# Weight loads on ScalarE's queue, and some normalisations on GpSimd, in a fused attention and gated-MLP kernel

## The chip, the cores and the metric

One core of one Trainium2 chip. The metric is the device time of one execution in microseconds (us), lower is better. The kernel before took 271.23 us (median of 3 runs, 269.55 to 272.23). TensorE is PE in the profile, its weight loads PEld, VectorE is DVE, ScalarE is ACT, GpSimd is POOL, and SyncE, which issues most transfers, is SP. A name with q (SPq, ACTq) is the engine's own instruction queue. A hole is a stretch in which TensorE has no matmul to run. An eviction copies a matmul's result out of psum, the accumulator. A crossbar transpose is a DMA transfer that transposes a tile on its way; here it brings a normalised tile from tring to xh, the input of the next matmuls. The clock is the share of TensorE's full clock that was granted.

## The reference, cut to what matters

```python
# x: 1 x 2048 x 448, bf16; 16 heads of 28; window of 8 keys, dilation 2
h  = x + attention(layernorm(x)) @ wo              # LN1, q/k/v, sliding window, wo
# gated MLP, F = 1792, Fh = 896
z  = gelu(layernorm(h) @ w_in)                     # LN2
z1 = z[..., :Fh]
z2 = layernorm(z[..., Fh:])                        # LN3, over 896
g  = einsum('ts,bsf->btf', w_sp, z2) + b_sp        # w_sp is 2048 x 2048
out = h + (z1 * g) @ w_out
```

There are three normalisations. LN1 and LN2 work on 16 blocks of 128 tokens by 448, LN3 on 16 blocks of 128 by 896. The last product with w_sp needs every block of LN3 before its first accumulation is complete.

## The kernel before

The program is a list of tasks with a duration, a priority and dependencies; a list scheduler (the planner) turns it into a fixed instruction order for each engine. A task may have `alts`: engines that can do it, each with a duration. The planner gives the task to whichever engine is free in its model.

```python
# planner, cut
if t.alts:
    for x in t.alts:
        ready[x].remove(t)
    t.eng = e
    t.dur = t.alts[e]
...
def ln_unit(u, which, src_deps, prio, ev_deps):      # LN1 and LN2: two blocks, u and u + 8
    ... # bn_stats, bn_aggr on VectorE
    tr = add("rs%d_%d" % (which, u), "pool", 1.05, em_r, deps=tb, prio=prio)   # 1/sqrt on GpSimd
    for n, b in enumerate(bl):
        def em_n(b=b, n=n):
            iss("dve", lambda e: e.tensor_scalar(tring[:, h[0], :]..., x_tm[:, b, :]...,
                     mv[:, b, 0:1], rs[:, b:b + 1], ALU.subtract, ALU.mult), ...)
        tn.append(add("nrm%d_%d" % (which, b), "dve", 0.41, em_n, ...))
    if which == 2 or u >= NPET:                      # crossbar transpose into xh
        return dma("sp", "tD%d_%d" % (which, u), lambda e: e.dma_start(
            xh[...], tring[:, h[0], :], transpose=True), ...)
...
t_wo.append(dma("sp", "wo%d" % hh, ...))             # 4 loads, one resource r_wo
ld_win(1, 2.0); ld_win(0, 2.4)                       # 8 loads, dma("sp", ...)
...
# LN3: rstd on GpSimd for a pair of blocks, then for each of the two
iss("dve", lambda e: e.tensor_scalar(z2p[:, b, :], z2p[:, b, :], mv3[:, b, 0:1], rs3[:, b:b + 1],
                                     ALU.subtract, ALU.mult), ...)
t_z2[b] = add("nrm3_%d" % b, "dve", 0.43, em, deps=[tp], ...)
...
pace = [by[n % i] for i in range(NT) for n in ("exp%d_0", "mask%d", "ot%d")]
chain(t_win[1] + t_win[0] + [t_wsp[b][0] for b in S_ORDER], pace)   # each load waits for a step and the load before
```

The softmax here doesn't subtract the row's maximum and nothing guards it: scores larger than these inputs give would overflow.

## Time and profile before

| | before |
|---|---|
| time, median | 271.23 us |
| profiled span, mean clock of the matmul engine | 270.2 us, 0.968 |
| PE / DVE / ACT / POOL busy | 250.4 / 150.5 / 88.5 / 33.5 us |
| first w_sp matmul | 149.51 us |
| PE idle from 8.76 to 149.5 us | 13.8 us |

A group line reads: source line, engine, operation, output <- inputs, shape, count, then busy us in all and mean ns of one, then the idle time of the engine just before. Kernel before, groups by form:

```profile
L668 DVE TENSOR_SCALAR tring<-x_tm,mv,rs 128x448 bf16<-128x448 bf16 x32 | 15.2, 492 | 4.3 <-POOL rs L648 4.3
L1033 DVE TENSOR_SCALAR z2p<-z2p,mv,rs 128x896 bf16<-128x896 bf16 x16 | 7.4, 501 | 1.1 <-POOL rs L648 1.1
L1084 PE MATMUL psum<-wspT_lo,z2p 128*128 128x512 bf16 x219 | 48.1, 379 | 0.4 <-issue 0.2
```

All 32 normalisations of LN1 and LN2 (line 668) and all 16 of LN3 (line 1033) run on VectorE at about 0.5 us each. None of them is on GpSimd. The first half of the w_sp matmuls (line 1084), which needs the results of LN3, is idle for 0.4 us in all.

### The profile page before, as it was taken

What the parts mean: (1) busy time and instruction counts of PE and PEld (TensorE: products, weight loads), DVE (VectorE), ACT (ScalarE), POOL (GpSimd) and SP (SyncE); (2) the same over time, 40 slices, a digit from 0 to 9 for tenths busy, and PEclk for the clock granted to TensorE, in tenths of its full rate; (3) what the DMA queues carried; (4) which work ended last, traced back from release to release, by engine and by line L of the source; (5) the groups of instructions that cost most, each with busy time, mean ns of one, the idle gap of its engine ahead of it and who ended that gap; (6) DMA issues with size and microseconds to landing.
All of it is one profiled execution on the core that took longest, in us unless ns stands there. A gap on an engine that the chain in (4) does not pass through costs nothing.

```text
span 270.2 us, 6513 instructions
## 1 busy us (share of the span) xinstructions
PE 250.4 (93%) x2912; PEld 126.0 (47%) x2922; DVE 150.5 (56%) x281; ACT 88.5 (33%) x97; POOL 33.5 (12%) x80
## 2 busy tenths in 40 slices
PE   7698967999969897989999999999999999999995
PEld 2275533445635444345555444444444444444442
DVE  3878861585784688599997133342334333334333
ACT  1458721737635745967667100000000000000000
POOL 7652200000211013113322000000000000000000
PEclk9979995999997999799999999999999999999999
DMA  7903495423275946659953434433000200010002
GB/s 207 281 26 66 102 166 107 109 53 70 67 103 115 98 96 75 114 101 168 222 87 80 77 86 95 90 80 107 0 0 2 68 0 0 2 51 17 0 2 68
DMA packets 55412, 22.03 MB, mean 82 GB/s; under 512 B 46664, under 2 KB 55256, under 8 KB 55384
## 3 DMA queue, kind: packets, MB, share of 16 engines
q1 hardware_dynamic: 54376, 20.40, 37.8%
q10 hardware_dynamic: 1008, 1.20, 1.6%
q8 instruction: 23, 0.38, 0.6%
q14 instruction: 5, 0.04, 0.1%
HBM read 8.39 MB, written 1.84 MB: 38 GB/s over the span
## 4 chain that ended last, share of the span: by engine, by line
PE 85%; DVE 4%; DMA 4%; POOL 3%; ACT 1%; issue 1%; POOLq 0%
PE psum L1084 36%; PE psum L790 11%; PE psum L988 9%; PE psum L1113 8%; PE psum L1047 8%; PE psum L830 5%; DMA xh<-tring 4%; PE psum L865 3%; PE psum L968 2%; PE psum L914 2%; ACT reg L642 1%; DVE reg L644 1%; DVE reg L932 1%; DVE tring L668 1%; PE psum L894 1%
## 5 line engine op out<-in xcount | busy, mean ns | idle before, releaser
L1094 DVE TENSOR_TENSOR ub<-psum,reg 128x512 bf16<-128x512 f32 x28 | 19.4, 692 | 68.9 <-PE psum L1084 68.9
L1084 PE MATMUL psum<-reg,z2p 128*128 128x512 bf16 x219 | 48.4, 379 | 0.3
L1084 PE MATMUL psum<-wspT_lo,z2p 128*128 128x512 bf16 x219 | 48.1, 379 | 0.4 <-issue 0.2
L1084 PEld LDWEIGHTS psum<-wspT_lo,z2p 128*128 128x128 bf16 x224 | 21.8, 98 | 26.6 <-issue 0.4
L1084 PEld LDWEIGHTS psum<-reg,z2p 128*128 128x128 bf16 x224 | 21.9, 98 | 26.3
L790 PE MATMUL psum<-xh,reg 64*128 64x128 bf16 (+3 forms) x336 | 29.6, 327 | 3.8 <-DMA xh<-tring 3.8
L988 PE MATMUL psum<-w_in,xh 64*128 64x448 bf16 x224 | 26.1, 380 | 5.0 <-DMA xh<-tring 3.5
L642 ACT ACTIVATE reg<-psum 128x896 bf16<-128x896 f32 (+5 forms) x23 | 18.7, 841 | 17.9 <-PE psum L747 6.5
L644 DVE CAST reg<-psum 128x896 bf16<-128x896 f32 (+4 forms) x14 | 15.1, 1076 | 14.0 <-PE psum L790 9.6
L878 ACT ACTIVATE reg<-psum 128x928 bf16<-128x928 f32 x18 | 16.9, 944 | 16.8 <-PE psum L865 7.4
L1113 PE MATMUL psum<-reg 128*128 128x448 bf16 x112 | 22.0, 352 | 0.0
L1047 PE MATMUL psum<-xh,w_in 64*128 64x512 bf16 x196 | 21.9, 376 | 0.0
L647 POOL TENSOR_SCALAR rs<-mv 128x2 f32<-128x2 f32 x24 | 7.8, 326 | 109.2 <-DVE mv L658 90.9
L790 PEld LDWEIGHTS psum<-xh,reg 64*128 64x128 bf16 x336 | 14.4, 99 | 14.5 <-issue 7.2
L657 DVE BATCH_NORM_STATS2 st<-x_tm 128x6 f32<-128x448 bf16 x32 | 19.5, 610 | 1.9 <-DMA x_tm<-in_A_x_dram 1.8
L988 PEld LDWEIGHTS psum<-w_in,xh 64*128 64x128 bf16 x224 | 11.8, 100 | 15.4 <-DMA xh<-tring 3.9
L668 DVE TENSOR_SCALAR tring<-x_tm,mv,rs 128x448 bf16<-128x448 bf16 x32 | 15.2, 492 | 4.3 <-POOL rs L648 4.3
L1019 DVE BATCH_NORM_STATS2 st<-z2p 128x6 f32<-128x448 bf16 x32 | 17.4, 598 | 0.0
L648 POOL TENSOR_TENSOR rs<-rs,nhalf 128x2 f32<-128x2 f32 x24 | 17.0, 708 | 2.0
L1057 ACT ACTIVATE reg<-psum 128x1024 bf16<-128x1024 f32 x14 | 14.3, 1024 | 7.2 <-PE psum L1047 7.2
L830 PE MATMUL psum<-reg,xh 64*64 64x448 bf16 x252 | 14.7, 373 | 1.6 <-DVE xh L644 1.0
L1113 PEld LDWEIGHTS psum<-reg 128*128 128x128 bf16 x112 | 11.0, 98 | 10.5
(65 smaller groups left out, 213.4 us busy)
## 6 DMA issues: line engine op xcount, KB each, us to landing
w_in<-in_B_w_in_dram SPq DMA_DIRECT2D x4, 448.0 KB, 5.2
out_dram<-tring SPq DMA_DIRECT2D x16, 112.0 KB, 1.7
x_tm<-in_A_x_dram SPq DMA_DIRECT2D x15, 112.0 KB, 6.1
w_in<-in_B_w_in_dram SPq DMA_DIRECT2D x4, 336.0 KB, 4.1
reg<-in_B_w_out_dram SPq DMA_DIRECT2D x1, 784.0 KB, 5.4
z2p<-in_A_wqkv_dram ACTq DMA_DIRECT2D x1, 672.0 KB, 4.9
reg<-in_B_b_sp_dram SPq DMA_DIRECT2D x1, 512.0 KB, 6.1
reg<-in_A_wqkv_dram ACTq DMA_DIRECT2D x1, 392.0 KB, 7.0
```

The lines of the kernel that those rows point to most:

```text
L642: iss("act", lambda e: e.activation(dst, src, AF.Copy), reads=rd, writes=wr)
L644: iss(eng, lambda e: e.tensor_copy(dst, src), reads=rd, writes=wr)
L657: iss("dve", lambda e: e.bn_stats(st[:, b, :], x_tm[:, b, :]), reads=[r_x[b]], writes=[rl[b]])
L668: iss("dve", lambda e: e.tensor_scalar(tring[:, h[0], :].rearrange("p (c s f) -> p s c f", c=NC7, s=2)[:, n], x_tm[:, b, :].rearrange("p ( ...
L790: iss("pe", lambda e, c=c, s=s, gi=gi, lhs=lhs: e.matmul(psum[:, bk[s] * 512 + cw * gi:bk[s] * 512 + cw * gi + cw], lhs, xh[64 * s:64 * s ...
L830: iss("pe", lambda e, c=c, s=s, w=w: e.matmul(psum[64 * w:64 * w + 64, bk[s] * 512:bk[s] * 512 + D], xh[64 * s:64 * s + 64, c, XO - HALO + ...
L988: iss("pe", lambda e, c=c, s=s: e.matmul(psum[:, zb[s] * 512:zb[s] * 512 + D], xh[64 * s:64 * s + 64, c, XO + 128 * u:XO + 128 * u + 128], ...
L1019: iss("dve", lambda e, b=b: e.bn_stats(st3[:, b, k, :], z2p[:, b, D * k:D * k + D]), reads=[r_z2[b][k]], writes=[r_st3[b][k]])
L1047: iss("pe", lambda e, c=c, s=s: e.matmul(psum[:, bk[s] * 512:bk[s] * 512 + 512], w_in[64 * s:64 * s + 64, c, 128 * f:128 * f + 128], xh[64 ...
L1084: iss("pe", lambda e, b=b: e.matmul(psum[:, gb[0] * 512:gb[0] * 512 + 512], z2p[:, b, 128 * f:128 * f + 128], src[:, b, 512 * (tc % 2):512 ...
L1094: iss("dve", lambda e: e.tensor_tensor(ub[:, us_[0], :], psum[:, gb[0] * 512:gb[0] * 512 + 512], bb[:, 512 * tc:512 * tc + 512], ALU.add), ...
L1113: iss("pe", lambda e, f=f: e.matmul(psum[:, wb[0] * 512:wb[0] * 512 + D], z1p[f][:, 128 * m:128 * m + 128], w_out[:, f, :], start=(f == 0) ...
```

## The change

Its intent is to keep SyncE's in-order queue free for the crossbar transposes that feed the matmuls: the wo and w_in loads are issued by ScalarE, wo is tracked as four parts, and the w_sp loads wait for a compute step only. In addition, normalisations may go to GpSimd, to relieve VectorE. The offsets and the seed of the planner were searched again, and it was told new issue times for the transposes (`issue=1.3`, `issue=1.2`, `bw=200.0`; not shown in the cut).

```diff
-MPEN = 5.115
-OFF = {"q": -60.45, ...}
-SEED, SIGMA = 953666, 1.0
+MPEN = 2.853
+OFF = {"q": -91.78, ...}
+SEED, SIGMA = 570774, 1.0
...
-        r_wo = Res("wo")
+        r_wo = [Res("wo%d" % i) for i in range(4)]
...
-                    t = dma("sp", "win%d_%d%d" ...
+                    t = dma("act", "win%d_%d%d" ...
...
-                    iss("dve", lambda e: e.tensor_scalar(tring...
+                    iss(tn[n].eng, lambda e: e.tensor_scalar(tring...
-                              acq=[] if n else [("tr", 1, h)]))
+                              acq=[] if n else [("tr", 1, h)], alts={"dve": 0.41, "pool": 0.65}))
...
-            t_wo.append(dma("sp", "wo%d" % hh, ...  prio=1.0 + 0.01 * hh, writes=[r_wo]
+            t_wo.append(dma("act", "wo%d" % hh, ... prio=-310 + 0.01 * hh, writes=[r_wo[hh]]
-        ld_win(1, 2.0); ld_win(0, 2.4)
+        ld_win(1, -300.0); ld_win(0, -299.0)
...
-                    iss("dve", lambda e: e.tensor_scalar(z2p[:, b, :], ...
+                    iss(tk[0].eng, lambda e: e.tensor_scalar(z2p[:, b, :], ...
-                t_z2[b] = add("nrm3_%d" % b, "dve", 0.43, ...)
+                t_z2[b] = add("nrm3_%d" % b, "dve", 0.43, ..., alts={"dve": 0.43, "pool": 1.05})
...
-        chain(t_win[1] + t_win[0] + [t_wsp[b][0] for b in S_ORDER], pace)
+        pace = [t_x[NB - 1]] + [by["mm%s1_%d" % (p, g)] for g in range(4) for p in "kq"]
+        chain(t_win[1] + t_win[0], pace, False)       # order in the plan only, no real wait
+        pace = [by[n % i] for i in range(2, NT) for n in ("exp%d_0", "mask%d", "ot%d")]
+        chain([t_wsp[b][0] for b in S_ORDER], pace)
```

With the durations 0.65 and 1.05 us, the planner put 24 of the 32 small normalisations and 8 of the 16 large ones on GpSimd.

More of the change, by code (lines that the diff above doesn't have):

```diff
@@ L35 @@
 WPEN = 200
-MPEN = 5.115
-OFF = {"q": -60.45, "v": -24.73, "evv": 46.46, "l": -68.6, "exp": 40.78, "mask": -30.77, "r": -72.61,
-       "o": -92.46, "ln": 28.79, "ot": 3.99, "y": 5.48, "h": 16.73, "ln2": -52.4, "zr": 73.75, "z2": 10.47,
-       "ge": -61.49, "n3": 62.79, "x0": -17.97, "xd": 1.56, "evq": 43.13}
-SEED, SIGMA = 953666, 1.0
+MPEN = 2.853
+OFF = {"q": -91.78, "v": -31.46, "evv": 70.84, "l": -101.63, "exp": 9.21, "mask": -63.08, "r": -105.01,
+       "o": -160.47, "ln": -77.16, "ot": -5.85, "y": -22.31, "h": -36.55, "ln2": -0.64, "zr": 155.82,
+       "z2": 10.2, "ge": -30.33, "n3": 78.44, "x0": -71.31, "xd": 55.9, "evq": 48.9}
+SEED, SIGMA = 570774, 1.0
 O_AFTER_LN = True
@@ L501, in bass_sequential_preLN__sliding_local_dilated__mixer_gmlp__prompt_kernel @@
         reg2_old = [r for rr in r_q + r_k for r in rr] + [r_qend, r_kend] + r_OT
-        reg3_old = [r_wo] + [r for e2 in r_E for r in e2] + r_L + r_V
+        reg3_old = r_wo + [r for e2 in r_E for r in e2] + r_L + r_V
         EP_TILE, EP_UNIT = {}, {}
@@ L571, in ld_win @@
                 for c0, c1 in ((0, 4), (4, 7)):
-                    t = dma("sp", "win%d_%d%d" % (z, s, c0), lambda e, s=s, c0=c0, c1=c1: e.dma_start(
+                    t = dma("act", "win%d_%d%d" % (z, s, c0), lambda e, s=s, c0=c0, c1=c1: e.dma_start(
                         w_in[64 * s:64 * s + 64, c0:c1, FH * z:FH * z + FH],
@@ L667, in em_n @@
                 def em_n(b=b, n=n):
-                    iss("dve", lambda e: e.tensor_scalar(tring[:, h[0], :].rearrange("p (c s f) -> p s c f", c=NC7, s=2)[:, n],
+                    iss(tn[n].eng, lambda e: e.tensor_scalar(tring[:, h[0], :].rearrange("p (c s f) -> p s c f", c=NC7, s=2)[:, n],
                                                          x_tm[:, b, :].rearrange("p (c f) -> p c f", c=NC7),
@@ L676, in ln_unit @@
                     xh[:, :, XO + 128 * u:XO + 128 * u + 128], tring[:, h[0], :], transpose=True), 128 * 896 * 2,
-                    deps=tn + list(ev_deps), prio=prio + 1.0 - 600, reads=LazyRes(r_tr, h), writes=[r_xh[u]], rel=[("tr", h)])
+                    deps=tn + list(ev_deps), prio=prio + 1.0 - 600, reads=LazyRes(r_tr, h), writes=[r_xh[u]], rel=[("tr", h)], issue=1.3, bw=200.0)
             bk = []
@@ L726, in bass_sequential_preLN__sliding_local_dilated__mixer_gmlp__prompt_kernel @@
                 t_xpad = add("evh", "dve", 0.17, em_e, deps=[th], prio=3.25, rel=[("ps", hb)])
-        c_wo0 = cst("c_wo0", [(lambda e: e.memset(wo_p[:, :, :], 0.0), [], [r_wo])], 1.65, prio=50, deps=[t_xh[1]])
+        c_wo0 = cst("c_wo0", [(lambda e: e.memset(wo_p[:, :, :], 0.0), [], r_wo)], 1.65, prio=50, deps=[t_xh[1]])
         def units(lo, hi):
@@ L938, in bass_sequential_preLN__sliding_local_dilated__mixer_gmlp__prompt_kernel @@
         for hh in range(4):
-            t_wo.append(dma("sp", "wo%d" % hh, lambda e, hh=hh: e.dma_start(
+            t_wo.append(dma("act", "wo%d" % hh, lambda e, hh=hh: e.dma_start(
                 wo_p[32 * hh:32 * hh + DH, :, :],
-                A_wo.rearrange("(g h d) n -> h d g n", g=4, h=4)[hh]), DH * 4 * D * 2, prio=1.0 + 0.01 * hh,
-                writes=[r_wo], deps=[c_wo0]))
-        ld_win(1, 2.0)
-        ld_win(0, 2.4)
+                A_wo.rearrange("(g h d) n -> h d g n", g=4, h=4)[hh]), DH * 4 * D * 2, prio=-310 + 0.01 * hh,
+                writes=[r_wo[hh]], deps=[c_wo0]))
+        ld_win(1, -300.0)
+        ld_win(0, -299.0)
         t_wsp = [[None, None] for _ in range(NB)]
@@ L950, in ld_wsp @@
                 dst[:, b, :], B_w_sp[1024 * half:1024 * half + 1024, 128 * b:128 * b + 128], transpose=True),
-                128 * 1024 * 2, prio=prio, deps=deps, writes=[r_wsp[b][half]] + list(extra))
+                128 * 1024 * 2, prio=prio, deps=deps, writes=[r_wsp[b][half]] + list(extra), issue=1.2)
         S_ORDER = [b for u in range(NU) for b in (u, u + 8)]
@@ L970, in em @@
                                                               start=(g == 0), stop=(g == 3)),
-                            reads=rot + [r_wo], writes=[r_bank[bk[s]]])
+                            reads=rot + r_wo, writes=[r_bank[bk[s]]])
             tm = add("mmy%d" % u, "pe", pe_n(D, 8), em, deps=t_ot[:tl_ + 1] + t_wo, prio=T + OFF["y"], acq=[("ps", 2, bk)], mode="F", nmm=8)
@@ L1031, in bass_sequential_preLN__sliding_local_dilated__mixer_gmlp__prompt_kernel, with em @@
             for b in (u, u + 8):
-                def em(b=b):
-                    iss("dve", lambda e: e.tensor_scalar(z2p[:, b, :], z2p[:, b, :], mv3[:, b, 0:1], rs3[:, b:b + 1],
+                tk = []
+                def em(b=b, tk=tk):
+                    iss(tk[0].eng, lambda e: e.tensor_scalar(z2p[:, b, :], z2p[:, b, :], mv3[:, b, 0:1], rs3[:, b:b + 1],
                                                          ALU.subtract, ALU.mult), reads=r_z2[b] + [r_ln3[b]], writes=r_z2[b])
-                t_z2[b] = add("nrm3_%d" % b, "dve", 0.43, em, deps=[tp], prio=T + OFF["n3"] + 0.4)
+                t_z2[b] = add("nrm3_%d" % b, "dve", 0.43, em, deps=[tp], prio=T + OFF["n3"] + 0.4, alts={"dve": 0.43, "pool": 1.05})
+                tk.append(t_z2[b])
         t_z1 = [[None] * FC7 for _ in range(2)]
@@ L1129, in bass_sequential_preLN__sliding_local_dilated__mixer_gmlp__prompt_kernel, with chain @@
         by = {t.name: t for t in pl.tasks}
-        def chain(loads, steps):
+        def chain(loads, steps, real=True):
             assert len(steps) >= len(loads)
@@ L1135, in chain @@
                 t.deps += loads[n - 1:n] if n else []
-                t.waits += [steps[n]] + (loads[n - 1:n] if n else [])
-                steps[n].mark = steps[n].mark or []
-        pace = [by[n % i] for i in range(NT) for n in ("exp%d_0", "mask%d", "ot%d")]
-        later = t_win[1] + t_win[0] + [t_wsp[b][0] for b in S_ORDER]
-        chain(later, pace)
+                if real and n:
+                    t.waits.append(steps[n - 1])
+                    steps[n - 1].mark = steps[n - 1].mark or []
+        pace = [t_x[NB - 1]] + [by["mm%s1_%d" % (p, g)] for g in range(4) for p in "kq"]
+        chain(t_win[1] + t_win[0], pace, False)
+        pace = [by[n % i] for i in range(2, NT) for n in ("exp%d_0", "mask%d", "ot%d")]
+        chain([t_wsp[b][0] for b in S_ORDER], pace)
         pace = [by["ge%d_%d" % (u, k)] for u in range(4, NU) for k in range(2)]
```

## The prediction

> **What bounds the kernel now.** I read the page's busy shares and slices first, then a table of stretches cut at the holes, then the timelines of TensorE and of the SyncE queue around those holes.
>
> ```profile
> PE 250.4 (93%) x2912; PEld 126.0 (47%) x2922; DVE 150.5 (56%) x281; ACT 88.5 (33%) x97; POOL 33.5 (12%) x80
> ...
> PE   7698967999969897989999999999999999999995
> ...
> PEclk9979995999997999799999999999999999999999
> ```
>
> TensorE carries the time: from slice 19 on (about 122 us) every slice is full and the clock is whole. The change can therefore gain only before that, and the PEclk row shows a second loss there: four slices at 0.5 to 0.7. The table of stretches (limits; length; busy us of PE, PEld, DVE, ACT, POOL; granted clock; DMA share; GB/s) puts both losses in the same places:
>
> ```profile
> 38.22:42.00 3.78, 0.00 (x0) 0.03 (x1) 0.83 (x1) 0.94 (x1) 0.00 (x0) 0.81 1.09 196
> 42.00:50.00 8.00, 8.00 (x106) 3.29 (x106) 2.35 (x2) 2.55 (x3) 0.00 (x0) 0.67 0.37 97
> 50.00:78.30 28.30, 27.94 (x720) 15.96 (x718) 19.77 (x25) 17.15 (x19) 2.66 (x4) 1.00 0.34 72
> 78.30:81.10 2.80, 0.06 (x8) 0.00 (x0) 2.80 (x5) 0.94 (x1) 0.00 (x0) 1.00 0.96 153
> 81.10:90.00 8.90, 8.89 (x174) 4.58 (x174) 4.46 (x9) 5.31 (x6) 0.93 (x2) 0.81 0.66 116
> 106.00:117.40 11.40, 8.69 (x116) 3.48 (x116) 8.59 (x15) 10.07 (x11) 2.19 (x4) 0.85 0.54 99
> 149.50:270.20 120.70, 117.35 (x550) 54.54 (x558) 41.18 (x72) 0.93 (x1) 0.00 (x0) 1.00 0.17 41
> ```
>
> Two holes of 3.78 and 2.74 us stand out, each followed by 8 to 9 us of full work at a clock of 0.67 and 0.81. TensorE's timeline names what ended the holes, and shows the slow clock in one group: the same 14 matmuls take 3.17 us right after the hole and 1.69 us later.
>
> ```profile
> 42.00 3.17 PE L790 MATMUL psum<-xh,reg 64*128 64x512 bf16 x14 [3.78 <-DMA xh<-tring]
> ...
> 48.51 1.69 PE L790 MATMUL psum<-xh,reg 64*128 64x512 bf16 x14
> ...
> 81.11 2.46 PE L988 MATMUL psum<-w_in,xh 64*128 64x448 bf16 x14 [2.75 <-DMA xh<-tring]
> ```
>
> Both waits are for a crossbar transpose that fills xh. The SyncE queue's timeline says why it was late:
>
> ```profile
> 21.10 1.92 SPq L675 DMA_TRANSPOSE xh<-tring  x1
> 23.06 6.76 SPq L939 DMA_DIRECT2D reg<-in_A_wo_dram  x4
> 29.87 0.63 SPq L572 DMA_DIRECT2D w_in<-in_B_w_in_dram  x1
> 30.54 2.57 SPq L675 DMA_TRANSPOSE xh<-tring  x1
> ...
> 72.44 5.23 SPq L949 DMA_TRANSPOSE wspT_lo<-in_B_w_sp_dram  x2
> 77.72 1.68 SPq L675 DMA_TRANSPOSE xh<-tring  x1
> ```
>
> The queue is in order. The second transpose of the first norm stands behind four wo loads that wait for one another (5.1 us of their 6.76 is waiting, by the queue's own waits), then behind w_in loads chained to attention steps; the last one goes out at 38.90 and lands at 41.87. At 72.44 the first transpose of the second norm, whose VectorE norms end at 73.7, stands behind two chained w_sp loads until 77.72.
>
> **What the Trainium skill says.** "TensorE: Matmul & The Clock Gate", Why this matters for your kernels: a TensorE idle gap beyond about 3 us drops the clock to half. The trace agrees, and shows it at 2.75 us too: 0.50 granted from 42.00 to 46.50, 0.58 from 81.1 to 83.6. So a hole costs nearly twice its length. "DMA: Bandwidth & Descriptors", Issuing engines are not separate DMA queues: another issuing engine saves sequencer time only, the transfers share 16 DMA engines. So I expect no faster transfers, only unblocked issue; mean DMA share is 0.34 to 0.66 in the stretches of interest, so there is room. "GPSIMD Engine Reference", 4.1 Engine selection: one-input elementwise work runs at roughly line rate there; the trace has no such GpSimd instruction of size, only memsets. "SBUF — State Buffer", Who interferes with whom: a VectorE instruction with two SBUF inputs and a GpSimd instruction that reads SBUF block each other fully. The trace agrees: a GpSimd instruction that usually takes 0.22 us took 1.03 us beside a mask multiply (first line GpSimd, second VectorE; both end at 70.5):
>
> ```profile
> 69.51 1.03 POOL L647 TENSOR_SCALAR rs<-mv 128x2 f32<-128x2 f32 x1 [37.87 <-DVE mv L658]
> ...
> 69.34 1.12 DVE L885 TENSOR_TENSOR reg<-reg,mband 128x1856 bf16<-128x1856 bf16 x1
> ```
>
> **The change, part by part.** The instruction orders of both kernels show what moved.
>
> (a) *SyncE queue.* The 4 wo and 8 w_in loads leave it, and the w_sp loads lose their waits for the load before; they wait for a compute step only. The five first-norm transposes now stand directly behind the x loads. When is the last one ready? GpSimd now does 11 of that norm's 14 remaining normalisations. Its second rsqrt pair began at 12.20. From there: 7 pairs of 1.02 us (12.20 to 13.22 in the timeline) are 7.1; one wo memset is 1.6; 11 norms. For one norm I take 0.22 us (the small tensor_scalar) plus 448 elements at 0.83 ns, the slope between the memsets of 128 (0.211) and 1792 elements (1.592): 0.59, with the gap 0.65, together 7.2. Sum 15.9, so 28.1 if it never waits. VectorE's last statistics ended at 30.5; they lose 11 norms of 0.49 in front of them but gain evictions. I take 30 to 31 for the last norm and 3.7 us for issue to landing (median of the xh transposes): about 34.5. TensorE reaches that group at 38.2. The hole of **3.78** goes, and with it the clock loss behind it, 8.00 x (1 - 0.67) = **2.64**.
>
> (b) *Second norm.* In the new order the two first output projections come right behind the last q/k group, and their gated-MLP matmuls a dozen groups later, so the queue and the order both give slack. The hole of **2.74** goes, and 8.89 x (1 - 0.81) = **1.69** of clock.
>
> (c) *End of attention, 106 to 117.4.* Idle is 11.40 - 8.69 = 2.71, clock loss 8.69 x 0.15 = 1.30, sum 4.0. Its named causes are a late mask and a late residual add on a crowded VectorE, and 0.75 us of a transpose. VectorE loses 24 norms of 0.492 (11.8 us) and 8 of 0.46 (the 896-element ones in the dense stretch; 3.7 us), but takes 7 evictions over from ScalarE (about 7 us). Net relief is 8 us over the kernel. I count half of the 4.0: **2.0**.
>
> (d) *What it adds.* ScalarE issues 12 loads: 8 of 0.61 us and 4 of 0.41 (6.76 less 5.1, by 4), 6.5 us in its in-order stream between the exps; the 7 evictions given away (0.9 us each) pay that back in total but not at each place. I charge a quarter on the path: **+1.6**. Moving a norm to GpSimd lengthens its chain by some 0.15 us per instruction and can collide with 9 masks of 1.1 us; transposes have slack of several us now, but a mask held up by a norm delays TensorE: **+0.6**. The eight 896-element norms (estimated 0.22 + 896 x 0.83 = 0.96 us) lie beside full TensorE stretches: 0.
>
> (e) *The last 120 us* have the same 448 + 112 matmuls at full clock: 0.
>
> Sum: 3.78 + 2.64 + 2.74 + 1.69 + 2.0 - 1.6 - 0.6 = 10.65. 271.2 - 10.7 = **260.5 us**, a ratio of 0.960.
>
> **Rivals.**
> (1) *The wait changes its name.* In-order ScalarE, with DMA issues between exps, becomes what attention waits on, and TensorE gets new holes of 1 to 2 us, with clock loss. For it: ScalarE is busy 10.07 of 11.40 us at 106 to 117.4. Against it: it is busy only 17.15 of 28.30 at 50 to 78.3, where most issues stand. Half of the gain would be lost: 265 to 267.
> (2) *Contention.* Unchained w_sp transposes and w_in loads fill the rings in front of xh transposes, so these land later though issued earlier. For it: landing already varies from 2.9 to 6.9 us. Against it: 3 to 4 us of slack in (a), more in (b). If only (a) held and (b) did not: 265.
> (3) *Everything falls into place.* All of (c) goes as well, and some of the 1.62 us idle at 90 to 106, and the charges of (d) hide: 255 to 257. For it: the changed offsets show that the order was searched again for this queue layout.
> (4) *GpSimd becomes the bound*, its norms arriving later than VectorE's did: 269 or more. Against it: 33.5 us busy before, plus 24 x 0.65 + 8 x 1.0 = 24 us more, is under 60 of 260.
>
> **Range and chances.** Steps (a) and (b) are worth 10.85 us together and I trust (a) most: 6.4 us alone passes 2% (5.4 us). The range runs from rival 3 with some left over to rival 1 or 2: 256 to 266.5. Faster by over 2% (below 265.8): 0.86; within 2%: 0.12; slower: 0.02, for it would need GpSimd or ScalarE to open holes larger than those closed.
>
> **What would show it.** (a) right: five xh transposes on the SyncE queue between 18 and 31 us with no load between, no hole before the first 128x512 q/k group, and that group near 1.7 us rather than 3.17. (b) right: no TensorE wait for an xh transpose over 1 us, and PEclk without a slice under 0.8 from slice 5 to 13. (c) right: idle and clock loss between the last q/k group and the end of attention under 6 us together. (d) right: DMA issues on ScalarE's queue near 0.4 to 0.6 us, GpSimd norms near 0.65 us, some of them over 1 us beside masks. (e) right: first w_sp matmul to the end within 1 us of 120.7. I would be wrong if TensorE's idle from 8.76 us to the w_sp stage, 13.7 us in all now (lengths less busy over all stretches of that table), stays above 10, or if half-clock slices reappear behind waits for ScalarE or GpSimd.

## The result, and the profile after

The changed kernel took **281.87 us** (median of 4 runs, 280.71 to 282.61) against 270.88 us of the kernel before in the same rounds: ratio 1.040 (95% interval 1.034 to 1.047), **slower**. Ratios here are the mean time of one kernel's fast runs over that of the other's fast runs of the same rounds, so not quite the ratio of the medians quoted. Executions over 1.5% slower than the fastest of the same kernel are left out of the means. The profiled spans are 280.9 and 270.2 us, a difference of 10.7.

The page of the changed kernel (busy time, then slices for PE, POOL and the clock):

```profile
PE 252.6 (90%) x2911; PEld 128.3 (46%) x2922; DVE 146.3 (52%) x257; ACT 81.5 (29%) x89; POOL 106.9 (38%) x112
...
PE   7569872999999999997996299999999999999995
...
POOL 7599992000288586499999800000000000000000
PEclk9997995799999999999999579999999999999999
```

There are two dips in PE: the 7th slice (about 42 to 49 us) and the 23rd (154 to 161 us). Both end a run of nines in the POOL row, and the clock drops with each. Attention in between is full. GpSimd went from 33.5 to 106.9 us busy: plus 73, where the prediction had counted plus 24. The groups say why:

```profile
L668 POOL TENSOR_SCALAR tring<-x_tm,mv,rs 128x448 bf16<-128x448 bf16 x24 | 46.6, 1943 | 2.5
L1035 POOL TENSOR_SCALAR z2p<-z2p,mv,rs 128x896 bf16<-128x896 bf16 x8 | 28.8, 3597 | 0.8
L1087 PE MATMUL psum<-wspT_lo,z2p 128*128 128x512 bf16 x219 | 51.4, 394 | 7.8 <-POOL z2p L1035 6.7
```

One normalisation takes 1.94 us (1.87 undisturbed) and 3.60 us on GpSimd, against 0.49 and 0.50 us on VectorE: four and seven times as long. The first w_sp matmuls, which had idled 0.4 us in all, idle 7.8 us, nearly all of it for the large ones (line 1087 here is line 1084 of the kernel before).

The first dip, as the timeline of GpSimd tells it (start, duration, engine, line, operation, shapes, count, idle before and what ended it):

```profile
12.63 0.23 POOL L647 TENSOR_SCALAR rs<-mv 128x2 f32<-128x2 f32 x1 [1.80 <-DVE mv L658]
...
34.07 0.23 POOL L647 TENSOR_SCALAR rs<-mv 128x2 f32<-128x2 f32 x1 [0.16 <-POOL tring L668]
34.39 0.72 POOL L648 TENSOR_TENSOR rs<-rs,nhalf 128x2 f32<-128x2 f32 x1
35.21 3.84 POOL L668 TENSOR_SCALAR tring<-x_tm,mv,rs 128x448 bf16<-128x448 bf16 x2
39.21 0.23 POOL L647 TENSOR_SCALAR rs<-mv 128x2 f32<-128x2 f32 x1 [0.16 <-POOL tring L668]
39.53 0.72 POOL L648 TENSOR_TENSOR rs<-rs,nhalf 128x2 f32<-128x2 f32 x1
40.35 3.84 POOL L668 TENSOR_SCALAR tring<-x_tm,mv,rs 128x448 bf16<-128x448 bf16 x2
```

GpSimd works from 12.63 to 44.19 us practically without a break. The SyncE queue and TensorE of the same kernel follow:

```profile
23.98 21.50 SPq L675 DMA_TRANSPOSE xh<-tring  x5
```

```profile
47.23 3.17 PE L790 MATMUL psum<-xh,reg 64*128 64x512 bf16 x14 [6.52 <-DMA xh<-tring]
```

The queue part did what it should: the five first-norm transposes go out with no load between them. But each now waits for its normalisation, so they still spread over 21.5 us, and the hole before the last q/k group grew from 3.78 to 6.52 us, with the same slow 3.17 us group behind it.

The second dip, on TensorE, and one large normalisation of the same stretch on GpSimd:

```profile
149.50 2.54 PE L1087 MATMUL psum<-wspT_lo,z2p 128*128 128x512 bf16 x11 [0.16 <-DVE mv L1025]
156.19 1.03 PE L1087 MATMUL psum<-wspT_lo,z2p 128*128 128x512 bf16 x2 [4.16 <-POOL z2p L1035]
157.93 0.61 PE L1087 MATMUL psum<-wspT_lo,z2p 128*128 128x512 bf16 x1 [0.71 <-DVE z2p L1035]
161.09 14.18 PE L1087 MATMUL psum<-wspT_lo,z2p 128*128 128x512 bf16 x54 [2.54 <-POOL z2p L1035]
```

```profile
157.43 3.60 POOL L1035 TENSOR_SCALAR z2p<-z2p,mv,rs 128x896 bf16<-128x896 bf16 x1
```

The w_sp stage starts at 149.50 us, as before (149.51). TensorE uses up what is normalised, and then waits three times for the rest; the last piece ends at 161.03, and TensorE goes on at 161.09. Eight pairs of LN3 follow one another on GpSimd from 122.02 us at 4.89 us a pair (0.23 + 0.72 for the square root, 3.60 for one block, 0.34 of gaps).

Where attention stood, the table of stretches of the changed kernel (limits; length; busy us and counts of PE, PEld, DVE, ACT, POOL; clock; DMA share; GB/s):

```profile
40.70:47.23 6.53, 0.01 (x4) 0.03 (x2) 0.84 (x1) 0.94 (x1) 3.39 (x2) 0.64 0.81 139
47.23:55.00 7.77, 7.77 (x104) 3.30 (x106) 2.35 (x2) 2.21 (x3) 0.00 (x0) 0.64 0.16 33
55.00:112.70 57.70, 56.93 (x1356) 33.61 (x1352) 47.02 (x61) 36.42 (x40) 28.01 (x23) 1.00 0.49 92
```

From 55 to 112.7 us there is 0.77 us of idle time at full clock. The hole of the second norm and the loss at the end of attention are gone.

After 149.5 us, same columns:

```profile
149.50:163.00 13.50, 6.09 (x19) 2.00 (x19) 2.18 (x5) 0.91 (x1) 10.83 (x7) 0.71 0.39 78
163.00:280.90 117.90, 114.51 (x531) 53.07 (x539) 40.04 (x70) 0.00 (x0) 0.00 (x0) 0.99 0.11 30
```

**The account.** Up to the w_sp stage the two kernels are even: TensorE idles 14.1 us from 8.76 to 149.5, against 13.8 before. What attention gained was spent in front of it, and on a new wait of 1.82 us for ScalarE at 129.90 us, behind it. The whole net loss lies after 149.5 us: 131.4 us against 120.7, which is 10.7. Of that, 7.4 us are more idle time (7.8 against 0.4) and 3.3 us are slower matmuls after the holes (219 at 394 ns against 379).

### The profile page after: what moved, and what is told of

Same layout as the page of the kernel before. It is cut to its first block, busy times and chain, and to the rows that moved or that the text cites. A ratio compares the mean times of both kernels' runs of the same rounds, so it can differ in the third digit from the quotient of the medians.

```text
span 280.9 us, 6555 instructions
## 1 busy us (share of the span) xinstructions
PE 252.6 (90%) x2911; PEld 128.3 (46%) x2922; DVE 146.3 (52%) x257; ACT 81.5 (29%) x89; POOL 106.9 (38%) x112
## 3 DMA queue, kind: packets, MB, share of 16 engines
q10 hardware_dynamic: 3432, 4.82, 7.3%
## 4 chain that ended last, share of the span: by engine, by line
PE 63%; POOL 23%; DVE 7%; issue 3%; POOLq 1%; DMA 1%
PE psum L1087 34%; POOL z2p L1035 8%; PE psum L1116 8%; POOL tring L668 7%; PE psum L790 6%; POOL rs L648 4%; PE psum L968 4%; PE psum L914 4%; PE psum L988 3%; PE psum L830 3%; PE psum L865 2%; DVE st L657 2%; DVE st L1019 1%; POOL rs L647 1%; DVE reg L644 1%
## 5 line engine op out<-in xcount | busy, mean ns | idle before, releaser
L1087 PE MATMUL psum<-wspT_lo,z2p 128*128 128x512 bf16 x219 | 51.4, 394 | 7.8 <-POOL z2p L1035 6.7
L668 POOL TENSOR_SCALAR tring<-x_tm,mv,rs 128x448 bf16<-128x448 bf16 x24 | 46.6, 1943 | 2.5
L644 DVE CAST reg<-psum 128x896 bf16<-128x896 f32 (+4 forms) x20 | 21.3, 1068 | 15.5 <-PE psum L790 13.9
L1035 POOL TENSOR_SCALAR z2p<-z2p,mv,rs 128x896 bf16<-128x896 bf16 x8 | 28.8, 3597 | 0.8
L988 PE MATMUL psum<-w_in,xh 64*128 64x448 bf16 x224 | 22.7, 350 | 1.8 <-ACT reg L1060 1.8
L647 POOL TENSOR_SCALAR rs<-mv 128x2 f32<-128x2 f32 x24 | 5.6, 232 | 46.2 <-DVE mv L658 43.3
L1050 PE MATMUL psum<-xh,w_in 64*128 64x512 bf16 x196 | 21.5, 376 | 0.0
L642 ACT ACTIVATE reg<-psum 128x896 bf16<-128x896 f32 (+5 forms) x17 | 13.4, 817 | 14.7 <-PE psum L790 6.8
L988 PEld LDWEIGHTS psum<-w_in,xh 64*128 64x128 bf16 x224 | 10.5, 94 | 11.7 <-issue 2.8
```

The source lines that it names most:

```text
L644: iss(eng, lambda e: e.tensor_copy(dst, src), reads=rd, writes=wr)
L668: iss(tn[n].eng, lambda e: e.tensor_scalar(tring[:, h[0], :].rearrange("p (c s f) -> p s c f", c=NC7, s=2)[:, n], x_tm[:, b, :].rearrange( ...
L988: iss("pe", lambda e, c=c, s=s: e.matmul(psum[:, zb[s] * 512:zb[s] * 512 + D], xh[64 * s:64 * s + 64, c, XO + 128 * u:XO + 128 * u + 128], ...
L1035: iss(tk[0].eng, lambda e: e.tensor_scalar(z2p[:, b, :], z2p[:, b, :], mv3[:, b, 0:1], rs3[:, b:b + 1], ALU.subtract, ALU.mult), reads=r_z ...
L1050: iss("pe", lambda e, c=c, s=s: e.matmul(psum[:, bk[s] * 512:bk[s] * 512 + 512], w_in[64 * s:64 * s + 64, c, 128 * f:128 * f + 128], xh[64 ...
L1087: iss("pe", lambda e, b=b: e.matmul(psum[:, gb[0] * 512:gb[0] * 512 + 512], z2p[:, b, 128 * f:128 * f + 128], src[:, b, 512 * (tc % 2):512 ...
```

## The experiments

Twelve kernels ran besides the change; each gave a correct result. Medians include slow runs, ratios do not, and medians of different rounds are not quite comparable (the kernel before had 267.96 to 270.88 in them). In short:

| run | what | median us | ratio to before, 95% |
|---|---|---|---|
| after | the change | 281.87 | 1.040 [1.034, 1.047] |
| e1_norms_on_dve | its plan, all normalisations issued on VectorE | 263.56 | 0.979 [0.971, 0.987] |
| e2_z2_on_dve | only the large ones back on VectorE | 271.32 | 1.009 [1.002, 1.016] |
| e3_ln_on_dve | only the small ones back on VectorE | 269.27 | 1.001 [0.991, 1.011] |
| e7_gpsimd_forms | GpSimd forms measured by themselves | (261.5, one run) | |
| e4_queue_only | before + queue part | 266.82 | 0.993 [0.985, 1.001] |
| e9_retune_only | before + new search numbers | 276.57 | 1.025 [1.017, 1.034] |
| e4b_queue_retune | before + both | 266.77 | 0.981 [0.971, 0.991] |
| e5_z2_pool_in_before | before + 8 large normalisations on GpSimd | 282.07 | 1.044 [1.035, 1.054] |
| e6_true_costs | the change, planner told 1.9 and 3.65 us | 262.97 | 0.981 [0.975, 0.986] |
| e8_late_loads | e4b with wo, w_in later | 266.09 | 0.989 [0.983, 0.995] |
| e8b_late_loads_afters_plan | e1 with wo, w_in later | 262.17 | 0.978 [0.974, 0.982] |
| e10_true_costs_late_loads | e6 with wo, w_in later | **261.26** | 0.974 [0.967, 0.981] |

The theory (G): GpSimd takes far longer for a normalisation than the plan and the prediction assumed, and its chain becomes what TensorE waits for. Rival 1: the load issues on ScalarE cost. Rival 2: the loads now share the DMA engines with the transposes. Rival 3: the new order is to blame.

### Normalisations back on VectorE: all, the large ones, the small ones

```diff
 # e1 (both lines); e2: only the second; e3: only the first
-                    iss(tn[n].eng, lambda e: e.tensor_scalar(tring...
+                    iss("dve", lambda e: e.tensor_scalar(tring...
-                    iss(tk[0].eng, lambda e: e.tensor_scalar(z2p...
+                    iss("dve", lambda e: e.tensor_scalar(z2p...
```

The plan, so the order of everything, stays that of the changed kernel.

> The changed kernel with its plan, queues and TensorE order untouched; only the 24 layer norms of 448 elements and the 8 of 896 that it puts on GpSimd are issued on VectorE, at the places where the plan has them. Theory G (GpSimd's slow normalisations, 1.87 and 3.60 us, are the whole loss): the hole of 6.53 us and the half clock behind it and the late start of the w_sp stage go, 257 to 264 us. Rival Q (loads on ScalarE's queue and unchained w_sp transposes cost as much as they gain): 268 us or more, with TensorE waiting for ScalarE or for xh transposes. Rival O (the newly searched order is the worse one): 268 or more with holes at other places.

> Only the 8 norms of 896 elements go back to VectorE. G: the last stage starts without its holes (4.16, 0.71 and 2.54 us and clock), 281.9 less about 10.7, 269 to 273 us; the hole of 6.5 us at the last q/k group stays. Q or O: unchanged within 2 us of 282.

> Only the 24 norms of 448 elements go back to VectorE; the 8 of 896 stay on GpSimd. G: no hole before the last q/k group, attention ends some 10 us earlier, but the chain of 8 pairs (rsqrt 1.2 and norm 3.6, 4.9 us each, 39 us) still ends the stage: 264 to 272 us, and TensorE waits for GpSimd at the start of the w_sp stage by more than in the changed kernel. Q or O: unchanged or slower.

Measured: 263.56 us with all of them back (fast runs 262.63 to 264.02, one slow run of 269.65), 271.32 with the large ones back, 269.27 with the small ones back (three fast runs within 0.3 us; two slow ones near 275.7). All of the loss, and more, belongs to the normalisations on GpSimd: the ratio falls from 1.040 to 0.979, some 16 us (18.3 by the medians of different rounds). The loads on ScalarE, the shared DMA engines and the new order are all still there in e1, so rivals 1 to 3 are not the cause of the loss. By the ratios, the large ones alone bring 3.1%, the small ones alone 3.9%, both 6.1%. Whether the two parts overlap is not shown: the missing 0.9% lies within the intervals. The traces show one way in which they would: in the changed kernel GpSimd comes out of the small ones of LN2 only at 122 us and then starts the large ones, so late small ones also push the large ones back; in e3 the first large one starts at 116.7 us (this from a slow profile, so only roughly comparable). In the same profile TensorE waits 3.5 us at the start of the w_sp stage, less than the 7.4 of the changed kernel, where more was expected.

In the profile of e2 the first hole stays and the w_sp stage has none; in that of e1 both are gone. TensorE of e2, then of e1:

```profile
47.20 3.04 PE L790 MATMUL psum<-xh,reg 64*128 64x512 bf16 x14 [6.50 <-DMA xh<-tring]
```

```profile
26.39 5.39 PE L790 MATMUL psum<-xh,reg 64*128 64x398 bf16 x42 [2.41 <-DMA xh<-tring]
...
120.64 2.82 PE L988 MATMUL psum<-w_in,xh 64*128 64x448 bf16 x28 [1.76 <-ACT reg L1060]
```

Then the first w_sp matmuls, again of e2 and of e1:

```profile
147.89 31.03 PE L1087 MATMUL psum<-wspT_lo,z2p 128*128 128x512 bf16 x141 [0.16 <-issue]
```

```profile
140.24 31.03 PE L1087 MATMUL psum<-wspT_lo,z2p 128*128 128x512 bf16 x141 [0.16 <-issue]
```

e1 still has a wait of 1.76 us for ScalarE, which had itself waited 5.17 us for the load of w_out, and one of 2.41 us for the first crossbar transpose, which had not been a hole in either kernel before; this one is taken up below.

### What does a normalisation cost on GpSimd by itself?

e7 is e1 with 27 more GpSimd instructions from 131.8 us on, just before and in the w_sp stage, where GpSimd has nothing else left to do: nine forms, three times each, into a scratch tile.

```diff
+        bench.append((lambda e: e.tensor_scalar(warm[:, 0:448], xs, sc, s2, ALU.subtract, ALU.mult), rd, [r_warm]))
+        bench.append((lambda e: e.tensor_scalar(warm[:, 0:448], xs, sc, None, ALU.subtract), rd, [r_warm]))
+        ...  # the same with immediates, 224 and 64 elements, fp32
+        bench.append((lambda e: e.tensor_copy(warm[:, 0:448], xs), rd, [r_warm]))
+        bench.append((lambda e: e.tensor_tensor(warm[:, 0:448], xs, xs, ALU.mult), rd, [r_warm]))
```

> The kernel of e1 with 27 GpSimd instructions appended in the w_sp stage, where GpSimd is idle: nine forms three times each, writing to a scratch tile, so the result stays right. If the 1.87 us is the instruction's own cost, the two-operation bf16 form of 448 elements with two pointer scalars takes 1.8 to 1.9 us here too. If it came from sharing a port with VectorE, it takes about 0.6 us here. The other forms tell what costs: one operation instead of two, immediates instead of pointers, a copy, two tensor inputs, 224 and 64 elements, fp32.

Groups of e7 (1138: both operations, scalars from memory, as in the kernel; 1139: one operation; 1140 and 1141: the same two with immediates; 1142: copy; 1143: product of two tiles; 1144: as 1138 with 224 elements):

```profile
L1138 POOL TENSOR_SCALAR warm<-x_tm,mv,rs 128x448 bf16<-128x448 bf16 x3 | 5.9, 1964 | 0.3
L1140 POOL TENSOR_SCALAR warm<-x_tm 128x448 bf16<-128x448 bf16 x3 | 5.1, 1715 | 0.3
L1139 POOL TENSOR_SCALAR warm<-x_tm,mv 128x448 bf16<-128x448 bf16 x3 | 4.4, 1458 | 0.3
L1141 POOL TENSOR_SCALAR warm<-x_tm 128x448 bf16<-128x448 bf16 x3 | 4.1, 1382 | 0.3
L1144 POOL TENSOR_SCALAR warm<-x_tm,mv,rs 128x224 bf16<-128x224 bf16 x3 | 3.6, 1196 | 0.3
L1143 POOL TENSOR_TENSOR warm<-x_tm 128x448 bf16<-128x448 bf16 x3 | 2.8, 934 | 0.3
L1142 POOL COPY warm<-x_tm 128x448 bf16<-128x448 bf16 x3 | 1.9, 640 | 0.2
```

The normalisation takes 1.86 to 2.10 us, 1.96 in the mean (expected: 1.8 to 1.9), so its length in the changed kernel is its own, not a lock or a wait. A copy of the same tile takes 0.64 us, close to the 0.59 us that the prediction had worked out from memsets. The operation is what makes the difference: a tensor_scalar with one operation costs 1.38 to 1.46 us, the second one another 0.3 to 0.5. From 224 to 448 elements the normalisation grows by 3.4 ns an element, where the estimate took 0.83. The estimate fits a copy, not this operation.

### Is it the order, or the queues? And does GpSimd alone make the loss?

```diff
 # e4: before, with the queue part, without alts for the normalisations, old search numbers
 # e9: before, with the new MPEN, OFF and SEED only
 # e4b: both
 # e5: before, and nothing else:
-                    iss("dve", lambda e: e.tensor_scalar(z2p[:, b, :], ...
+                    iss("pool" if b >= 8 else "dve", lambda e: e.tensor_scalar(z2p[:, b, :], ...
```

> The kernel before with the queue part of the change alone: wo and w_in loads issued by ScalarE, wo in four parts, w_sp loads without waits for the load before; no norm may go to GpSimd, and the old search numbers for the order are kept. Theory (the queue part is good, the GpSimd norms undo it): faster than before, 260 to 265 us, no hole over 1 us before the last q/k group or at the first gated-MLP group. Rival (the gain of the all-VectorE variant came from the newly searched order, not from the queues): within 1% of before, 268 to 272.

> The kernel before with only the new search numbers for the order; queues and engines as before. Theory: 268 to 276 us, so no gain, as the numbers were searched for other queues. Rival (the order is what gains): under 266.

> Queue part and the new search numbers, planned without GpSimd norms (unlike the variant that kept the changed kernel's plan and only issued the norms on VectorE). Theory: 259 to 264 us, near the 263.6 of that variant. Rival (the plan made with GpSimd norms is what gives the speed): over 266.

> The converse test: the kernel before, with the 8 second norms of the 896-element pairs issued on GpSimd and nothing else changed. If these norms at 3.6 us each are what costs the changed kernel its 10 us at the end, this gives 279 to 285 us with holes in the w_sp stage that wait for GpSimd. If the loss in the changed kernel needs its other parts too (its later start of the gated MLP), 271 to 274.

Measured: 266.82, 276.57, 266.77 and 282.07 us. The theory missed on e4: its median is 1.8 us above the range, and its interval includes no gain. It missed on e4b too, whose median is 2.8 us above its range and above the 266 of its rival; its spread is wide (263.0 and 265.1 in its fast runs, 268.4 and 269.8 in two that count as slow), so that rival stays open. The two that carry the queue part are faster in the mean (0.993, 0.981) and the new order alone on the old queues is slower by 2.5%. The two parts together have 1.9% (0.9 to 2.9), on two fast runs. So rival 3 falls as a cause of the loss with the new queues; whether the searched order gains with them is not shown, for the intervals of e4 and e4b overlap.

e5 is the converse of e2 and the clearest of the runs: every second normalisation of LN3 changed its engine, in the kernel before, and 12 us are lost. Its profile fell in a slow run (span 286.6), so the durations are not compared, but the waits have the same names as in the changed kernel:

```profile
156.66 0.39 PE L1084 MATMUL psum<-wspT_lo,z2p 128*128 128x512 bf16 x1 [1.91 <-POOL z2p L1033]
158.39 0.61 PE L1084 MATMUL psum<-wspT_lo,z2p 128*128 128x512 bf16 x1 [1.35 <-DVE z2p L1033]
161.54 0.61 PE L1084 MATMUL psum<-wspT_lo,z2p 128*128 128x512 bf16 x1 [2.54 <-POOL z2p L1033]
163.28 0.61 PE L1084 MATMUL psum<-wspT_lo,z2p 128*128 128x512 bf16 x1 [1.12 <-DVE z2p L1033]
166.43 30.57 PE L1084 MATMUL psum<-wspT_lo,z2p 128*128 128x512 bf16 x127 [2.54 <-POOL z2p L1033]
```

### Is GpSimd wrong for this work, or was the plan given a wrong number?

```diff
-  alts={"dve": 0.41, "pool": 0.65}))
+  alts={"dve": 0.41, "pool": 1.9}))
-  alts={"dve": 0.43, "pool": 1.05})
+  alts={"dve": 0.43, "pool": 3.65})
```

> The changed kernel with the planner told what the norms cost on GpSimd, 1.9 and 3.65 us in place of 0.65 and 1.05, so that it chooses with true numbers; it still gives 11 to 16 of the small norms and 5 of the large ones to GpSimd. If the wrong cost in the plan is what made the loss, 262 to 268, under before. If any of these norms on GpSimd costs, 268 to 275.

Measured: 262.97 us (261.37 to 264.52, four fast runs), a ratio of 0.981 in place of 1.040, from two numbers in the source (18.9 us between medians of different rounds). The planner still gives 19 small (expected: 11 to 16) and 5 large normalisations to GpSimd, at the same cost each:

```profile
L668 POOL TENSOR_SCALAR tring<-x_tm,mv,rs 128x448 bf16<-128x448 bf16 x19 | 37.3, 1961 | 2.0
L1035 POOL TENSOR_SCALAR z2p<-z2p,mv,rs 128x896 bf16<-128x896 bf16 x5 | 18.0, 3594 | 0.5
```

```profile
139.46 31.25 PE L1087 MATMUL psum<-wspT_lo,z2p 128*128 128x512 bf16 x144
```

GpSimd is busy 87.6 us here, and the w_sp stage starts at 139.46 us and has no hole over 0.6 us. So the slow engine, off the critical path, costs nothing that can be measured here. It cost in the changed kernel because the plan expected its results a long time before they came; that fewer of them went there in e6 (24 in place of 32) is part of the same correction. Against e1, where GpSimd does none of them, this is the same time within the spread.

### Do the moved loads delay the transposes?

The hole of 2.41 us in e1 waits for a transpose that went out at 21.43 us and landed 4.82 us later. From 20 to 30 us the DMA share is 1.03. The loads were therefore planned later in ScalarE's stream:

```diff
-        pace = [t_x[NB - 1]] + [by["mm%s1_%d" % (p, g)] for g in range(4) for p in "kq"]
+        for t in t_wo:
+            t.deps.append(by["mmk1_2"])
+        pace = [by["mm%s2_%d" % (p, g)] for g in range(4) for p in "kq"]
         chain(t_win[1] + t_win[0], pace, False)
```

> The queue part with the new search numbers and no GpSimd norms, and the wo and w_in loads planned later in ScalarE's stream (wo behind the third group of chunk 1, w_in behind the groups of chunk 2), so that the first crossbar transposes of the first norm do not share the DMA engines with them. Theory (sharing the engines is what makes the first transpose land late, 4.8 us after issue and 9.4 in a slow run): the first transpose lands within 3.5 us, the hole of 1.7 to 2.4 us before the first 64x398 group is under 0.7, and the time is 258 to 262. Rival (the wait is for the norm and not for the transfer, or other traffic takes the place): 262 to 267, hole unchanged.

> The same later loads, in the changed kernel with its plan and all norms issued on VectorE. Theory: 259 to 263, and less spread between runs than without the later loads. Rival: no better than the 263.6 measured without them.

> The best two put together: the changed kernel, planned with the true GpSimd costs, and with the wo and w_in loads planned later in ScalarE's stream. If the two small waits for crossbar transposes that the true-cost run still has (0.67 and 1.43 us) come from loads that share the DMA engines, they go and the time is 259 to 262. Rival: the plan shifts elsewhere and the time stays 262 to 265.

Measured: e8 266.09, e8b 262.17, e10 261.26 us. The stretch of 20 to 30 us, first of e1, then of e8b, same columns as above:

```profile
20.00:30.00 10.00, 7.59 (x144) 4.58 (x142) 9.83 (x22) 4.32 (x5) 4.38 (x7) 0.83 1.03 156
```

```profile
20.00:30.00 10.00, 8.21 (x238) 4.83 (x232) 9.83 (x23) 7.14 (x8) 4.38 (x7) 1.00 0.37 72
```

In e8b the DMA share falls from 1.03 to 0.37, the median landing time of the transposes issued from 20 to 28 us from 5.0 to 2.9 us, and the wait for the transpose goes. In this pair the loads delay the transposes. That they are the whole cause is not shown: in e8 no wo or w_in load is issued before 31.33 us, and the first transpose still takes 4.7 us to land, where 3.5 was expected (TensorE does not wait for it there, in its other order). Nor is a gain shown. e8b's ratio of 0.978 lies inside the interval of e1's 0.979, and e8 is not faster than e4b (fast runs 263.7 to 267.4, against 263.0 and 265.1), so there the expectation failed. A later load shifts the whole plan: e8b waits 1.79 us for a mask in place of the transpose, and from 20 to 40 us TensorE idles 2.39 us in it and 2.41 in e1. The clock loss of e1 does not speak for the later loads either, for e7, which has e1's loads and the same wait, has none:

```profile
26.49 3.71 PE L790 MATMUL psum<-xh,reg 64*128 64x398 bf16 x42 [2.49 <-DMA xh<-tring]
```

What can be said of e8b is that its six runs were all fast and within 2.3 us of one another.

The two together, e10, are the fastest kernel: 261.26 us, six fast runs between 259.81 and 262.96, a gain of 2.6% (1.9 to 3.3) over before and some 6% under the changed kernel by the ratios. Its interval does not part it from e6 or e1. No wait of TensorE after 26 us is longer than 0.6 us in its profile.

## Why the prediction was wrong

It said 260.5 us and got 281.87; it gave 2% to "slower". **The step that failed is the duration of a normalisation on GpSimd**, in (a) "0.22 us (the small tensor_scalar) plus 448 elements at 0.83 ns, the slope between the memsets": 0.59 us, measured 1.87; and in (d) 0.96 us for the large ones, measured 3.60. A memset has no input and no arithmetic, and the slope between memsets (0.83 ns an element) did not carry over to an operation with two arithmetic steps (3.4 ns). The Trainium skill's "GPSIMD Engine Reference", 4.1 Engine selection, on which the prediction drew, pointed the same way with its rough line rate for one-input work, and so did the 0.65 us written in the source. The prediction said itself that the trace had no such instruction of size: three numbers agreed, and none of them was a measurement.

Step by step:

- **(a) The SyncE queue.** The mechanism held: five transposes with no load between. The sum did not: 15.9 us predicted from the first square-root pair to the last normalisation, 31.6 measured (12.63 to 44.19). The 11 normalisations took 21.0 in place of 7.2 (13.8 of the 15.7 us excess), the rest is gaps and waits of 0.16 us between dependent instructions. Last transpose predicted at 34.5, TensorE went on at 47.23. Both terms, +3.78 and +2.64, became -2.74 (the hole grew to 6.52) and about 0 (7.77 x 0.36 = 2.8 us of clock loss again). That "a hole costs nearly twice its length" did not hold in general: this one cost 1.4 times its length, and the 2.49 us of e7 no clock at all.
- **(b) The second norm.** Right: no wait for a transpose over 1 us from 55 to 112.7 us, and the clock whole.
- **(c) End of attention.** Right and more: 0.77 us idle over the whole stretch. Eight evictions went to VectorE, not 7.
- **(d) Costs.** The ScalarE issues are as said (0.60 us for a w_in load, 0.33 to 0.59 for a wo load), and no hole waits for them. The collision with a mask came as said: two small normalisations took 4.71 us beside a mask, in place of 3.84. The 0 for the large normalisations failed. At the estimated 0.96 us a pair would have taken some 2.2 us (4.89 - 3.60 + 0.96), and eight pairs from 122.0 would have been done near 140, before the stage begins; at 3.60 they end at 161.0.
- **(e) The last stage** was to be within 1 us of 120.7 and took 131.4, for that reason. The start of the stage did not gain the 10 us either.
- **The rivals.** Rival 4 is what came: "GpSimd becomes the bound, its norms arriving later than VectorE's did: 269 or more". It was set aside with a busy share, "under 60 of 260". That was the wrong argument twice: the busy time was 106.9, and a share of the span says nothing of a chain that must end before a stage may start. Rival 2 was found in a small form in e1, as the wait of 2.41 us. The prediction had seen room in a DMA share of 0.34 to 0.66, but its own table has 1.09 and 0.96 in the two holes. Rival 1 was not seen in attention; the 1.82 us for ScalarE at 129.90 come after it, where ScalarE had waited 5.23 us for the load of w_out, not for its own issues.
- **What would have shown it** was named well: "GpSimd norms near 0.65 us", and the idle time of TensorE up to the w_sp stage staying "above 10" (it is 14.1).

A good part of the predicted gain was there to be had: with true durations, and the loads planned later, e10 has a ratio of 0.974, where the prediction said 0.960.

## What to carry to other kernels

Before work is moved to another engine, measure that very operation there (one extra instruction into a scratch tile in an idle stretch is enough); do not scale it from another operation. Where a planner chooses engines by durations written in the source, a duration that is too short by a factor of three can be worse than no choice at all (1.040 against e1's 0.979), for the plan then builds on results that come late: correcting two numbers took this kernel from 1.040 to 0.981 of the time before. And a lightly loaded engine is not safe by its share; ask when its chain starts, how long one link is, and which stage needs the last one.

## What the Trainium skill lacked or had wrong

- "GPSIMD Engine Reference", 4.1 Engine selection, puts one-input elementwise work at roughly line rate on GpSimd. For tensor_scalar this did not hold: 1.87 us (undisturbed) for 128x448 bf16 with two operations against 0.49 us on VectorE, 3.60 against 0.50 for 128x896; one operation 1.38 to 1.46. A copy took 0.64. The page would help with such a table by operation.
- "TensorE: Matmul & The Clock Gate", Why this matters for your kernels, names an idle gap of about 3 us. Here no single length decided: the same 42 matmuls of 64x398 took 5.39 us after a gap of 2.41 (e1), and 3.71 after one of 2.49 (e7) as after one of 0.15 in the changed kernel. So the figure is no safe bound.
